# GpSimd's order in the attention written out, table scatters one to a round, and the first expert's weights split by VectorE

## The chip, the core and the metric

The kernel runs on one core of a Trainium2 chip. The metric is the device time of the core in microseconds, start to end; the median of three runs counts. The engines are TensorE (PE, with its weight loads listed as PEld), VectorE (DVE), ScalarE (ACT), GpSimd (POOL) and SyncE (SP), which here issues DMAs.

## The reference

```python
def _attn_ref(q, k, v):                     # each [8, 8, 576, 64]
    scores = scale * np.matmul(q, k.transpose(0, 1, 3, 2))
    mask = (pos // 64)[:, None] >= (pos // 64)[None, :]
    scores = np.where(mask, scores, -1000000000.0)
    attn = softmax(scores)
    return np.matmul(attn, v)
...
def _moe_ref(x, w_gate, w_output_gate, w1, w2):   # x [4608, 512], 8 experts
    logits = x @ w_gate
    e_idx = np.argmax(logits, axis=1)
    gate_w = softmax(logits)[rows, e_idx]
    eom = 1.0 / (1.0 + np.exp(-(x @ w_output_gate)))
    for e in range(E):
        mask = e_idx == e
        h = np.maximum(x[mask] @ w1[e], 0.0)      # 512 -> 1024
        ye = h @ w2[e]                            # 1024 -> 512
        out[mask] = gate_w[mask, None] * eom[mask, e, None] * ye
```

The attention's output, with the heads of a token side by side, is x. Each token goes to one expert, the one with the largest logit.

## The kernel before

**Attention.** The 8 batches of 8 heads are 32 pairs of heads, four to a batch. A pair is worked through in a software pipeline of 138 rounds (`NG`), four rounds to a pair; `round_of(g)` emits what each round holds: maxima for pair g // 4, exponentials for the pair one back, values for the pair two back, and the norm and turn of the pair three back. Float32 products are made of 16-bit halves. So a probability tile (`pc`, and `pcr` for the odd 64 rows) has a low part (`lpc`, `lpcr`, L258, in `lows`), and V a high and a low part (`vh` by ScalarE, `vl` by GpSimd, L152). GpSimd makes the low parts, one `lpcr`, five blocks of `lpc` and one `vl` to a pair; TensorE's value matmuls (L267 to L269) read them.

**Routing.** When a batch's x is there, `finish_batches` is put on the list `later`. It is a generator with the logits (L532 to L541), the largest one and its one-hot `oh` (L550 to L560), the place in the expert's queue (a matmul, L577 to L588), the slot `sli` and the gate `idg` (L599). At the end stands one scatter per 128 tokens, `tab_d<-idg,sli`, an indirect DMA issued by GpSimd (L604), which writes token number and gate to the table in HBM. `pay_later` takes a generator one step on in a round whose letter it yielded; None means any. Batches 0 and 1, 2 and 3, 4 and 5 are routed as joint groups of ten 128-token tiles, 6 and 7 alone, with five each.

**First expert.** `load_first`, put on `later` in round 120, loads the first expert's w1 and w2 in chunks. It reads the ids of the first tokens from the table (`fetch_ids`, L783, behind all scatters of the batches 0 to 5), gathers their rows of x (`fetch_x`, L794, into `xg`), and splits the weights into halves (`split`, L822 by ScalarE for the high part, L824 for the low part). `split` cuts a low part into quarters unless VectorE makes it. In rounds of `FIRST`, and behind the attention, the generator `ahead` is taken a step on: staging of tokens (L893 to L895), and h steps, the matmuls by w1 (L946).

**What sets the order.** Within `tc.manual_schedule` TensorE, ScalarE and VectorE work in the order in which the code emits; GpSimd and the DMA queues are ordered by a scheduler, from what its operations depend on. Behind the attention the experts' loop runs for the rest of the time.

Of the kernel before, what the change touches and what calls it, by code (L numbers as in the profile page):

```python
# [26 lines left out]
def block_attention_top1_moe(  # L27
# [11 lines left out]
    nc = tc.nc  # L39
    B, H, S, D = q.shape  # L40
# [459 lines left out]
    def pay_later(kind=None):  # L500
        for g in list(later):
            if kind is None or want.get(g) in (None, kind):
                want[g] = next(g, later)
                if want[g] is later:
                    later.remove(g)

    scatters, tab_reads = [], []
    GROUPS, Ls = ((0, 1), (2, 3), (4, 5), (6,), (7,)), {}
    ROUNDS = "ywab"

    def finish(b, xT):
        group = next(x for x in GROUPS if b in x)
        if b == group[0]:
            L = small.tile([P, len(group), NT, 16], F32, name="L", padded_shape=[P, 2, NT, 16])
            Ls[group] = L
        later.append(finish_batches(b, group, Ls[group], xT))

    def finish_batches(b, group, L, xT):

        n, b0 = len(group), group[0]  # L520
        joint = n > 1
        M = n * NT

        def tile_(shape, dt, name):
# [78 lines left out]
        for t in range(M):  # L603
            sc = nc.gpsimd.indirect_dma_start(  # L604
                out=tab_d, out_offset=IOA(ap=sli[:, t:t + 1].bitcast(U32), axis=0),
                in_=idg[:, b0 + t // NT, t % NT, :], in_offset=None, bounds_check=TROWS - 1, oob_is_err=False,
            ).ins
            if scatters:
                tc.declare_no_dep(sc, group="scatters", reason="distinct slots")
            for ins in tab_init + tab_reads:  # L610
                tc.add_manual_dep(sc, ins.name, SYNC, reason="after earlier accesses of the table")
            tc.add_to_no_dep_group("scatters", sc)
            scatters.append(sc)
            if b < B - 4:
                yield ROUNDS[t % 4]
            elif t % 2:
                yield


    def counts(col, name):  # L620
# [13 lines left out]
    def route_first():  # L634


        cnt = counts(B - 2, "cnt0")
        mx = small.tile([P, 1], F32, name="f_mx")
        nc.vector.tensor_reduce(mx, cnt, AX.X, ALU.max)
        eq = small.tile([P, E], F32, name="f_eq")  # L640
        nc.vector.scalar_tensor_tensor(eq, cnt, mx, erev, ALU.is_equal, ALU.mult)
        er = small.tile([P, 1], F32, name="f_er")
        nc.vector.tensor_reduce(er, eq, AX.X, ALU.max)
        nc.vector.tensor_scalar(first, erev, er, None, ALU.is_equal)
        fe = small.tile([P, 1], F32, name="f_e")
        nc.vector.tensor_scalar(fe, er, -1.0, float(E), ALU.mult, ALU.add)
        nc.vector.tensor_copy(f_i, fe)
        nc.vector.tensor_scalar(fe, fe, float(NTOK), None, ALU.mult)
        nc.vector.tensor_scalar(row0, t64[:, 0:8:2], fe, None, ALU.add)
# [4 lines left out]
    def sequence(order, i0, used):  # L654
        seq = []
        for i, kind in enumerate(order):
            k = KINDS.index(kind)
            seq.append((BKIND[k] + used[k], KTILES[k], i0 + i))
            width[i0 + i] = KROWS[k] // KTILES[k]
            used[k] += 1  # L660
        return seq

    used = [0] * len(KINDS)
    steps = sequence(ORDER, 0, used)
# [100 lines left out]
    @contextmanager  # L765
    def chain():
        if chained[0] is None:
            yield
        else:
            with tc.issue_after(chained[0].ins):  # L770
                yield


    def fetch_ids(st, halves=None):

        c, n, i = st
        if i not in ids:
            ids[i] = fs.tile([P, 2, 2], I32, name="ids", bufs=8)
        lo, hi = halves or (0, n)
        row = row0[0:1, 2 * c + lo:2 * c + lo + 1] if i < 2 else rti[0:1, c:c + 1]  # L780
        with tc.issue_after(read[0].ins) if read[0] else nullcontext():
            rv = nc.gpsimd.value_load(row, min_val=0, max_val=E * NTOK)
            read[0] = nc.gpsimd.dma_start(  # L783
                ids[i][:, lo:hi], tab_d[bass.ds(rv, P * (hi - lo)), :].rearrange("(h p) c -> p h c", p=P)
            )
        for sc in scatters:
            tc.add_manual_dep(read[0].ins, sc.name, SYNC, reason="after the scatters")
        tab_reads.append(read[0].ins)

    def fetch_x(st, halves=None):  # L790
        c, n, i = st
        for h in range(*(halves or (0, n))):
            nx = NTOK - 2 * S if 2 * i + h < 3 else NTOK
            nc.gpsimd.indirect_dma_start(  # L794
                out=xg[i % NXG][0:width[i], h], out_offset=None, in_=x_d[0:nx, :],
                in_offset=IOA(ap=ids[i][0:width[i], h, 0:1].bitcast(U32), axis=0), bounds_check=nx - 1, oob_is_err=False,
            )

    def rows_of(w, ev, j):

        n = 1024 // w.shape[2]
        rows = w.rearrange("e (g p) n -> e p g n", p=P)[bass.ds(ev, 1), :, n * j:n * (j + 1)]
        return rows.rearrange("e p g n -> (e p) g n")

    def quarter(w, t):
        return t.rearrange("p (g n) -> p g n", n=w.shape[2])
# [40 lines left out]
    def load_first():  # L847

        route_first()
        with chain():  # L850
            ev = nc.sync.value_load(f_i[0:1, 0:1], min_val=0, max_val=E - 1)

        wc = {}

        def load(w, c):
            dt, nm = ((F16, "hh"), (BF16, "hl"))[c % 2]
            wc[c] = fs.tile([P, KF, 2, P], dt, name=nm).rearrange("p f h n -> p (f h n)").bitcast(F32)
            nc.sync.dma_start(quarter(w, wc[c]), rows_of(w, ev, c))

        for c in range(4):  # L860
            load(w1, c)
        for r in "bwyab":
            yield r
        assert len(scatters) == (B - 2) * NT
        fetch_ids(steps[0])
        fetch_ids(steps[1], (0, 1))
        fetch_x(steps[0])
        fetch_x(steps[1], (0, 1))
        yield "w"
        for w, fn in ((w1, split_w1), (w2, split_w2)):  # L870
            for c in range(4):
                with tc.issue_after(last_exp[0].ins):
                    fn(nc.gpsimd, 0, wc[c], c)
                if w is w1:
                    load(w2, c)
                yield "yabw"[c]

    def buf(i):
        return 0 if i < 2 else (i - 1) % 2
# [179 lines left out]
    def round_of(g):  # L1059

        r = g % 4

        def do(back, name, *args):
            p, rr = divmod(g - back, 4)
            if 0 <= p < NPR:
                getattr(pairs[p], name)(*args)

        if r == 0:
            if g < 4 * NPR:
                max_odd(g // 4)  # L1070
            do(0, "max_tile", 0)
            do(4, "prob_tile", 3)
            do(12, "norm")
            do(4, "lows", 3)
        elif r == 1:
            do(5, "prob_tile", 0)
            do(5, "prob_tile", 1)
            do(1, "max_tile", 1)
            do(5, "lows", 0)
            do(5, "lows", 1)  # L1080
            if g == 4 * NPR + 9:
                turn_rest(NPR - 1, NPR)
        elif r == 2:
            do(6, "prob_tile", 2)
            do(10, "values_odd")
            do(2, "max_tile", 2)
            do(2, "max_rest")
            pay_later("m")
            pay_later("n")
            do(10, "values", 0)  # L1090
            pay_later("v")
            do(6, "lows", 2)
        else:
            do(-5, "turn")
            if g < 4 * NPR:
                turn_max(g // 4)
            if g < 4 * NPR + 8:
                turn_rest(g // 4 - 3, g // 4 + 2)
            pay_later("x")
            do(11, "values", 1)  # L1100
        for fn in events.get(g, ()):
            fn()
        pay_later("abwy"[r])

    NG = 4 * NPR + 10
    FIRST = range(NG - 6, NG)
    AT = mybir.EngineType
    with tc.manual_schedule(engines={AT.PE, AT.Activation, AT.DVE}):
        for g in range(NG):
            round_of(g)  # L1110
            if g in FIRST:
                next(ahead)
        while later:
            next(ahead, None)
            pay_later()
# [112 lines left out]
```

## Time and profile before

| what | value |
|---|---|
| runs | 821.64, 818.17, 815.3 us; median 818.17 us |
| profiled execution | 816.6 us, span 815.0 us |
| TensorE | 725.2 us busy, 89% of the span, mean granted clock 0.948 |
| VectorE, ScalarE, GpSimd | 533.8, 445.3, 415.5 us busy |

The attention takes about the first 400 us of the span. Busy shares are means over stages; the rows below are taken by stage. In a timeline's row stand the start, the duration, the engine, the line, the operation and its operands, the number of like instructions that the row joins, and in brackets the idle time ahead of it, with what ended it ("issue": nothing that the profile shows).

### The profile page before, as it was taken

The page shows a single profiled execution, that of the slowest core. Times are in us where ns is not written, and L with a number is a line of the kernel's source. Part 1 is how long each engine was busy: PE and PEld are TensorE (multiplying, and loading weights), DVE is VectorE, ACT ScalarE, POOL GpSimd, SP SyncE. Part 2 cuts the span into 40 slices and gives each one's busy share as a digit, 9 for nine tenths or more (in the row PEclk, how much of TensorE's full clock was granted, in tenths as well). Part 3 has the DMA queues.
Part 4 walks back from the last instruction along what each step waited for, and adds up shares of the span by engine and source line. Part 5 has one row for each costly group of instructions (what it writes and reads, how often), then busy time and mean ns, then how long its engine had stood idle before and what let it go on. Part 6 is the DMA issues. An engine that isn't in the chain of part 4 may idle for free. (4 is left out here: it accounts for less than half of the span.)

```text
span 815.0 us, 24272 instructions
## 1 busy us (share of the span) xinstructions
PE 725.2 (89%) x9879; PEld 536.3 (66%) x9879; DVE 533.8 (65%) x889; ACT 445.3 (55%) x630; POOL 415.5 (51%) x411
## 2 busy tenths in 40 slices
PE   5899998679985998976997799999999999999994
PEld 4687877458762777745874576956668566686651
DVE  7677778637784577727353796967678666796530
ACT  2676665346661665515220776855577655885530
POOL 3788787768867786459424644222333332220011
PEclk9999999979997899968798999999999999999998
DMA  6555655424544254325107799789999969941601
GB/s 155 130 132 139 143 135 123 105 53 116 144 102 90 62 131 101 103 64 157 31 1 250 179 264 305 240 254 308 322 303 353 314 167 297 229 112 43 230 27 43
DMA packets 207850, 131.61 MB, mean 161 GB/s; under 512 B 161552, under 2 KB 180016, under 8 KB 207728
## 3 DMA queue, kind: packets, MB, share of 16 engines
q1 hardware_dynamic: 199680, 110.66, 49.7%
q0 software_dynamic: 8048, 19.29, 7.6%
q8 instruction: 80, 1.31, 0.7%
q14 instruction: 42, 0.34, 0.2%
HBM read 127.08 MB, written 19.34 MB: 180 GB/s over the span
## 5 line engine op out<-in xcount | busy, mean ns | idle before, releaser
L946 PEld LDWEIGHTS <-w1b 128*128 128x128 f16 (+1 forms) x2208 | 177.1, 98 | 22.6 <-DVE w1b L824 1.1
L946 PE MATMUL ps_s<-xt,w1b 128*128 128x256 f16 (+5 forms) x1920 | 175.4, 253 | 0.8 <-issue 0.4
L975 PE MATMUL ps_o<-w2b,hh 128*128 128x512 f16 (+1 forms) x560 | 169.4, 384 | 4.4 <-ACT hh L954 4.4
L824 DVE TENSOR_TENSOR w2b<-w2f,w2b 128x1024 bf16<-128x1024 f32 x80 | 92.9, 1221 | 90.1 <-ACT w2b L822 75.9
L258 POOL TENSOR_TENSOR lpc<-pc 128x512 f16<-128x512 f32 x143 | 144.1, 1041 | 3.9 <-ACT pc L249 2.7
L984 POOL DMA_INDIRECT out_dram<-ys,ids x38 | 51.8, 1362 | 153.2 <-ACT ys L983 82.5
L178 DVE TENSOR_REDUCE nmz<-ps_s 128x2 bf16<-128x896 f32 (+3 forms) x128 | 82.6, 692 | 48.7 <-PE ps_s L194 47.2
L975 PE MATMUL ps_o<-w2b,hl 128*128 128x512 f16 x280 | 107.6, 384 | 0.2 <-DVE hl L955 0.2
L975 PEld LDWEIGHTS <-hh 128*128 128x128 f16 x560 | 55.2, 99 | 68.0 <-ACT hh L954 4.5
L824 DVE TENSOR_TENSOR w1b<-w1f,w1b 128x1024 bf16<-128x1024 f32 x80 | 92.8, 1219 | 1.5 <-ACT w1b L822 0.8
L983 ACT ACTIVATE ys<-ps_o,ids 128x512 f32<-128x512 f32 (+1 forms) x38 | 26.1, 686 | 111.8 <-PE ps_o L975 91.5
L249 ACT ACTIVATE pc<-ps_s 128x1024 f32<-128x1024 f32 (+1 forms) x96 | 78.4, 882 | 12.5 <-PE ps_s L213 12.4
L822 ACT CAST w1b<-w1f 128x1024 f16<-128x1024 f32 x80 | 78.4, 1045 | 4.4 <-DMA w1f<-in_moe_w_dram 4.3
L258 POOL TENSOR_TENSOR lpcr<-pcr 128x640 f16<-128x640 f32 x32 | 40.1, 1253 | 78.1 <-ACT pcr L249 78.1
L129 DVE TENSOR_TENSOR tr<-ps_s,tr 128x1024 f16<-128x1024 f32 (+1 forms) x62 | 47.1, 769 | 49.1 <-ACT tr L128 46.0
L822 ACT CAST w2b<-w2f 128x1024 f16<-128x1024 f32 x80 | 77.8, 1043 | 1.6 <-DMA w2f<-in_moe_w_dram 1.6
L794 POOL DMA_INDIRECT xg<-x_d,ids x38 | 54.3, 1429 | 36.6 <-DVE xr L908 12.7
L213 PE MATMUL ps_s<-tr,tr 64*128 64x512 f16 (+3 forms) x512 | 63.5, 314 | 9.6 <-issue 9.3
L249 ACT ACTIVATE pcr<-ps_s 128x640 f32<-128x640 f32 x32 | 22.5, 705 | 87.4 <-PE ps_s L241 42.4
L128 ACT CAST tr<-ps_s 128x1024 f16<-128x1024 f32 (+1 forms) x62 | 41.5, 670 | 41.9 <-PE ps_s L124 41.9
L187 PE MATMUL ps_s<-tr 64*128 64x384 f16 (+3 forms) x256 | 38.0, 314 | 26.7 <-DVE tr L129 22.2
L213 PEld LDWEIGHTS <-tr 64*128 64x128 f16 x768 | 35.4, 98 | 38.8 <-issue 28.0
(215 smaller groups left out, 1582.2 us busy)
## 6 DMA issues: line engine op xcount, KB each, us to landing
w1f<-in_moe_w_dram SPq DMA_DIRECT2D x80, 512.0 KB
w2f<-in_moe_w_dram SPq DMA_DIRECT2D x80, 512.0 KB
nat<-in_k_dram SPq DMA_DIRECT2D x64, 128.0 KB
nat<-in_q_dram SPq DMA_DIRECT2D x64, 128.0 KB
vn<-in_v_dram SPq DMA_DIRECT2D x64, 128.0 KB
x_d<-xn SPq DMA_DIRECT2D x32, 256.0 KB
vn<-in_v_dram SPq DMA_DIRECT2D x64, 32.0 KB
hh<-in_moe_w_dram SPq DMA_DIRECT2D x4, 512.0 KB
```

Of the source, the lines that this page charges most:

```text
L128: (hi or nc.scalar.copy)(th, ps)
L129: nc.vector.tensor_tensor(tl, ps, th, ALU.subtract)
L178: last_max[0] = nc.vector.tensor_reduce(o, ps[:, :, c0:c1], AX.X, ALU.max, negate=True)
L213: nc.tensor.matmul(os[ab], ks(kc, ab), qs(qc, ab), start=j == 0, stop=j == 3)
L249: last_exp[0] = nc.scalar.activation(self.pt[i], ap, AF.Exp, scale=SCALE)
L258: eng.tensor_tensor(self.pl[i][:, sl], self.pt[i][:, sl], self.high(i)[:, sl], ALU.subtract)
L794: nc.gpsimd.indirect_dma_start(out=xg[i % NXG][0:width[i], h], out_offset=None, in_=x_d[0:nx, :], in_offset=IOA(ap=ids[i][0:width[i], h, 0 ...
L822: nc.scalar.copy(hi, src)
L824: eng.tensor_tensor(lo[at], src[at], hi[at], ALU.subtract)
L946: nc.tensor.matmul(ph[:, f4].rearrange("p (h n) -> p h n", n=w), wv[:, cc, f, :], xv[:, cc], start=(k == 0), stop=(k == 3 * KD - 1))
L975: nc.tensor.matmul(py, hv[:, f, h], wv[:, f, :], start=(k == 0), stop=(k == 3 * KF - 1))
L984: nc.gpsimd.indirect_dma_start(out=out, out_offset=IOA(ap=ids[i][0:w, h, 0:1].bitcast(U32), axis=0), in_=ys[0:w], in_offset=None, bounds_c ...
```

## The change

- GpSimd is put under `tc.manual_schedule`, so its work in the attention stands in the order of the code.
- A scatter's generator yields a letter after every scatter: "abw" in turn, so one scatter in three of the four rounds of a pair (batch 5: "yabw", one in every round).
- Batches 4 and 5 are no longer one group; they are routed apart, with the letters of a joint group.
- `load_first` waits one round longer and fetches the ids; the low parts of the first expert's weights are made by VectorE, two to a round-letter's step, in whole chunks; the gathers `fetch_x` come after the first two chunks of w1.
- `FIRST` has four rounds instead of six: 132, 133, 136 and 137.

```diff
-    GROUPS, Ls = ((0, 1), (2, 3), (4, 5), (6,), (7,)), {}
-    ROUNDS = "ywab"
+    GROUPS, Ls = ((0, 1), (2, 3), (4,), (5,), (6,), (7,)), {}
...
-        joint = n > 1
+        joint = b < B - 2
...
-            if b < B - 4:
-                yield ROUNDS[t % 4]
-            elif t % 2:
-                yield
+            yield ("yabw"[t % 4] if b == B - 3 else "abw"[t % 3]) if joint else None
...
-        for r in "bwyab":
+        for r in "bwyabw":
             yield r
         assert len(scatters) == (B - 2) * NT
         fetch_ids(steps[0])
         fetch_ids(steps[1], (0, 1))
-        fetch_x(steps[0])
-        fetch_x(steps[1], (0, 1))
-        yield "w"
         for w, fn in ((w1, split_w1), (w2, split_w2)):
             for c in range(4):
                 with tc.issue_after(last_exp[0].ins):
-                    fn(nc.gpsimd, 0, wc[c], c)
+                    fn(nc.vector, 0, wc[c], c)
                 if w is w1:
                     load(w2, c)
                 yield "yabw"[c]
+                if w is w1 and c == 1:
+                    fetch_x(steps[0])
+                    fetch_x(steps[1], (0, 1))
...
-    FIRST = range(NG - 6, NG)
+    FIRST = (NG - 6, NG - 5, NG - 2, NG - 1)
-    with tc.manual_schedule(engines={AT.PE, AT.Activation, AT.DVE}):
+    with tc.manual_schedule(engines={AT.PE, AT.Activation, AT.DVE, AT.Pool}):
```

Line numbers behind L508 are smaller by one to four in the changed kernel: the scatter is L603, the ids read L779, the gather L790, the split L820.

GpSimd in the pairs 13 and 14, where batches 0 and 1 are scattered (`lpc` and `lpcr` are low parts, `vl` the low V, L604 the scatters), before:

```order
L258 TENSOR_TENSOR lpcr<-pcr 128x640
L258 TENSOR_TENSOR lpc_3770<-pc_3766 128x512 x2
L258 TENSOR_TENSOR lpc_3771<-pc_3767 128x512 x2
L258 TENSOR_TENSOR lpc_3772<-pc_3768 128x512
L152 TENSOR_TENSOR vl_104<-vn_99,vh_102 128x640
L604 DMA tab_d<-idg,sli 37120x2 x10
L258 TENSOR_TENSOR lpcr<-pcr 128x640
```

and now:

```order
L258 TENSOR_TENSOR lpcr<-pcr 128x640
L258 TENSOR_TENSOR lpc_3770<-pc_3766 128x512 x2
L258 TENSOR_TENSOR lpc_3771<-pc_3767 128x512 x2
L603 DMA tab_d<-idg,sli 37120x2
L258 TENSOR_TENSOR lpc_3772<-pc_3768 128x512
L152 TENSOR_TENSOR vl_104<-vn_99,vh_102 128x640
L258 TENSOR_TENSOR lpcr<-pcr 128x640
L603 DMA tab_d<-idg,sli 37120x2
L258 TENSOR_TENSOR lpc_4051<-pc_4047 128x512 x2
L258 TENSOR_TENSOR lpc_4052<-pc_4048 128x512 x2
L603 DMA tab_d<-idg,sli 37120x2
L258 TENSOR_TENSOR lpc_4053<-pc_4049 128x512
```

The ten scatters in a row have become single ones between low parts; the first has moved ahead of the pair's last low part and low V.

GpSimd at the attention's end, from the gathers (L794, now L790) on, before:

```order
L794 DMA xg_8327<-x_d,ids 128x512 x2
L794 DMA xg_8329<-x_d,ids 128x512
L152 TENSOR_TENSOR vl_103<-vn_98,vh_101 128x128
L824 TENSOR_TENSOR w1b_8325<-hh,w1b_8325 128x256 x4
L824 TENSOR_TENSOR w1b_8325<-hl,w1b_8325 128x256 x4
L258 TENSOR_TENSOR lpcr<-pcr 128x640
L824 TENSOR_TENSOR w1b_8325<-hh,w1b_8325 128x256 x4
L824 TENSOR_TENSOR w1b_8325<-hl,w1b_8325 128x256 x4
L152 TENSOR_TENSOR vl_104<-vn_99,vh_102 128x128
L824 TENSOR_TENSOR w2b_8326<-hh,w2b_8326 128x256 x4
```

and now, from the second ids read (L779) on:

```order
L779 DMA ids<-tab_d 128x2
L258 TENSOR_TENSOR lpcr<-pcr 128x640
L790 DMA xg_8379<-x_d,ids 128x512 x2
L790 DMA xg_8381<-x_d,ids 128x512
L778 TENSOR_LOAD row_199
L778 ISA x2
L152 TENSOR_TENSOR vl_104<-vn_99,vh_102 128x128
L603 DMA tab_d<-idg,sli 37120x2 x10
```

The weight quarters are gone from GpSimd, and the gathers have moved behind the last `lpcr`.

VectorE at the routing of one of the last batches, before:

```order
L541 TENSOR_REDUCE L<-ps_s 128x80
L301 TENSOR_SCALAR sm<-ps_v 128x10
L302 RECIPROCAL sm<-sm 128x10
L305 TENSOR_TENSOR xn<-ps_v,sm 128x2x2x64 x2
L305 TENSOR_TENSOR xn<-ps_v,sm 128x128
L550 TENSOR_REDUCE mx<-L 128x5
L553 TENSOR_TENSOR eq<-L,mx 128x40
```

and now:

```order
L820 TENSOR_TENSOR w1b_8377<-hh,w1b_8377 128x1024
L820 TENSOR_TENSOR w1b_8377<-hl,w1b_8377 128x1024
L540 TENSOR_REDUCE L<-ps_s 128x80
L301 TENSOR_SCALAR sm<-ps_v 128x10
L302 RECIPROCAL sm<-sm 128x10
L305 TENSOR_TENSOR xn<-ps_v,sm 128x2x2x64 x2
L305 TENSOR_TENSOR xn<-ps_v,sm 128x128
L820 TENSOR_TENSOR w1b_8377<-hh,w1b_8377 128x1024
L820 TENSOR_TENSOR w1b_8377<-hl,w1b_8377 128x1024
L549 TENSOR_REDUCE mx<-L 128x5
L552 TENSOR_TENSOR eq<-L,mx 128x40
```

Two low parts of whole chunks now stand ahead of the logits' sum (L540), and two ahead of the largest logit (L549).

## Rows read from the trace of the kernel before

**Rows 1.** The page's slices of 20.4 us: TensorE's busy tenths, granted clock.

```profile
PE   5899998679985998976997799999999999999994
...
PEclk9999999979997899968798999999999999999998
```

**Rows 2.** Windows: length, busy time (instructions) of PE, PEld, DVE, ACT, POOL, clock.

```profile
66.91:95.98 29.07, 27.58 (x624) 22.62 (x620) 20.91 (x44) 18.94 (x31) 22.97 (x21) 1.00 0.58 139
124.32:135.49 11.17, 9.13 (x210) 7.67 (x206) 10.36 (x23) 6.13 (x10) 7.66 (x8) 1.00 0.47 112
145.42:190.69 45.27, 32.31 (x624) 24.36 (x620) 24.52 (x50) 18.94 (x31) 32.80 (x31) 0.85 0.36 81
169.44:180.98 11.54, 10.87 (x209) 8.76 (x210) 5.87 (x11) 6.59 (x11) 7.65 (x7) 0.81 0.15 34
241.50:286.40 44.90, 33.20 (x624) 24.51 (x620) 24.53 (x50) 18.94 (x31) 32.71 (x31) 0.85 0.39 82
337.18:356.34 19.16, 13.36 (x208) 8.52 (x206) 8.66 (x31) 4.70 (x9) 9.50 (x10) 0.87 0.54 156
356.34:372.00 15.66, 15.46 (x165) 12.70 (x164) 3.67 (x8) 6.55 (x11) 10.21 (x13) 0.61 0.20 52
388.00:400.00 12.00, 11.55 (x84) 10.33 (x83) 5.19 (x18) 3.72 (x7) 9.45 (x13) 0.53 0.11 27
404.43:407.21 2.78, 2.78 (x30) 2.31 (x31) 0.08 (x1) 1.72 (x3) 0.00 (x0) 1.00 0.08 17
```

**Rows 3.** Timeline of GpSimd in a quiet pair, and the next pair's start.

```profile
66.91 1.25 POOL L258 TENSOR_TENSOR lpcr<-pcr 128x640 f16<-128x640 f32 x1 [1.28 <-ACT pcr L249]
68.22 5.04 POOL L258 TENSOR_TENSOR lpc<-pc 128x512 f16<-128x512 f32 x5
73.22 1.40 POOL L152 TENSOR_TENSOR vl<-vn,vh 128x640 f16<-128x640 f32 x1
75.89 1.25 POOL L258 TENSOR_TENSOR lpcr<-pcr 128x640 f16<-128x640 f32 x1 [1.28 <-ACT pcr L249]
```

**Rows 4.** Timeline of GpSimd: the first two and the last of ten scatters.

```profile
153.69 1.05 POOL L604 DMA_INDIRECT tab_d<-idg,sli  x1 [0.56 <-DVE idg L599]
155.05 1.01 POOL L604 DMA_INDIRECT tab_d<-idg,sli  x1 [0.30 <-issue]
...
165.30 0.97 POOL L604 DMA_INDIRECT tab_d<-idg,sli  x1 [0.30 <-issue]
```

**Rows 5.** Timeline of TensorE and ScalarE during these scatters.

```profile
163.59 0.62 PE L213 MATMUL ps_s<-tr,tr 64*128 64x512 f16 x2 [1.50 <-issue]
...
168.65 0.70 ACT L249 ACTIVATE pcr<-ps_s 128x640 f32<-128x640 f32 x1 [16.27 <-remote]
```

**Rows 6.** Timeline: a scatter after the third burst, value matmuls beside it and later.

```profile
357.75 1.00 POOL L604 DMA_INDIRECT tab_d<-idg,sli  x1 [0.16 <-DMA tab_d<-idg,sli]
...
359.49 4.53 PE L291 MATMUL ps_v<-vn,pc 128*128 128x65 f32 x20
...
391.04 4.53 PE L291 MATMUL ps_v<-vn,pc 128*128 128x65 f32 x20
```

**Rows 7.** Timeline of VectorE, GpSimd and TensorE from 372 us on.

```profile
372.89 13.75 DVE L553 TENSOR_TENSOR eq<-L,mx 128x40 f32<-128x40 f32 x1
377.10 2.34 PE L291 MATMUL ps_v<-vn,pc 128*128 128x65 f32 x20
384.05 2.54 POOL L824 TENSOR_TENSOR w2b<-hl,w2b 128x256 bf16<-128x256 f32 x4
...
387.52 0.21 PE L577 MATMUL ps_s<-oh,below 128*128 128x40 f16 x1 [8.08 <-DVE oh L560]
...
411.07 0.20 DVE L553 TENSOR_TENSOR eq<-L,mx 128x40 f32<-128x40 f32 x1
...
435.09 1.08 PE L893 MATMUL ps_o<-ident,xg 128*128 128x128 f32 x4 [5.62 <-DMA xg<-x_d,ids]
```

**Rows 8.** Timeline of TensorE: the first matmul of a pair that reads a low V.

```profile
77.64 0.21 PE L268 MATMUL ps_v<-vl,pcr 64*128 64x64 f16 x2
```

**Rows 9.** Groups by line: VectorE's low parts of expert weights, busy and mean ns.

```profile
L824 DVE TENSOR_TENSOR w1b<-w1f,w1b 128x1024 bf16<-128x1024 f32 x80 | 92.8, 1219 | 1.5 <-ACT w1b L822 0.8 <-issue 0.6
```

## The prediction

> **What bounds the kernel now.** I read the slices first. TensorE (PE) is the busy engine nearly everywhere, and there are dips: slices 7 and 8 (143 to 183 us), 12 and 13, 17 and 18, and 21 and 22 [rows 1]. The first three fall in the attention, and the granted clock of TensorE falls beside them. The windows put sizes to them. Three quiet pairs take 29.07 us, with TensorE busy for 27.58 of them; the same number of matmuls takes 45.27 and 44.90 us where the routing of batches 0 and 1, and of 2 and 3, ends; 19.16 us go by in what is one pair at batches 4 and 5 [rows 2]. Then I read GpSimd. In a quiet pair it computes the low parts for 7.7 us (1.25 + 5.04 + 1.40) of a cadence of 8.98 us and waits 1.28 us for ScalarE [rows 3]: it is close behind, and not the bound. In the long pairs it issues table scatters back to back, 0.97 to 1.05 us each, 0.30 us apart [rows 4].
>
> While they run, TensorE all but stops. Its gaps are marked "issue", no wait that the trace shows, and are up to 1.50 us; when it goes on, ScalarE's exponentials, 16.27 us late, hold it up once more [rows 5]. What stops it I can't read. It isn't scatters as such: with two more scatters after the third burst the same 20 value matmuls took 4.53 us, as they did 30 us later with no scatter, both at the low clock [rows 6]. So the burst, beside a dense stream of small matmuls, is what the stall goes with.
>
> The fourth dip in the attention is another thing. GpSimd subtracts weight quarters back to back to 386.6 us, and one 128x40 subtraction on VectorE, 0.20 us elsewhere, takes 13.75 us; it ends when GpSimd pauses. TensorE, done at 379.4 us, waits 8.08 us for the one-hot behind it [rows 7]. After both kinds of stall the clock is low: 0.61 of full speed over 356 to 372 us and 0.53 over 388 to 400 us [rows 2].
>
> The Trainium skill, "SBUF — State Buffer", "Who interferes with whom", says that a VectorE instruction with two SBUF inputs and a GpSimd instruction that reads SBUF lock each other out for one whole instruction. By that the wait would be at most one quarter, 0.64 us (2.54 for four); the row says 13.75 us, some 20 quarters, so the measurement decides here.
>
> **The change, part by part.** The sum is made against the profiled execution, 816.6 us (span 815.0, 1.6 around it), which lies 0.2% under the median, 818.17.
>
> *Scatters of batches 0 to 3.* They stand one to a round, three to a pair, between low parts. The three pairs from 145.42 us take 45.27 us. Without a stall I put them at 29.07 us plus what routing adds to a pair, 11.17 less 8.98, so 2.2: together 31.2 us [rows 2, 3]. 14.1 us are lost there, and 44.90 less 31.2, 13.7 us, at the second burst.
>
> What takes the stall's place is GpSimd's lag. Its work in these pairs is 22.97 us [rows 2] plus 10 scatters at 1.15 us (one with a gap of 0.15, half of the 0.30), 11.5 us. The first scatter now also stands before the last low part of pair 13 and waits there for the gates: GpSimd gets to it at about 150.7 us (145.42 + 1.25 + four parts of 1.01), the scatter started at 153.69 [rows 4], so 2.9 us, and queued behind it are the last low part, the low V and the next pair's. Sum: 37.4 us of GpSimd against 31.2 us. Of the 6.2 us, the low parts' slack takes 3.0: the low V is done at 74.62 us, and the first matmul that reads one comes at 77.64 [rows 3, 8]. 3.1 to 3.2 us become waits of TensorE. **Gain: 14.1 + 13.7 - 2 x 3.15 = 21.5 us.** (From 29.07 as the unhindered time it would be 25.7, and 19 if the routing costs twice as much.)
>
> *Batches 4 and 5*, now routed apart. The pair with the third burst takes 19.16 us against 9.7, the mean of the three quiet ones: 9.5 lost. The low clock after it has TensorE busy in 15.46 of 15.66 us at 0.61: 0.39 x 15.66 / 0.5 is 12.2 us at half speed, of which half, 6.1, would be saved; I take 5.5, for some of it is not matmul rate. Against that stand batch 4's own routing, 2.2 us at the price above, and a lag of 5 scatters to a batch, about 1. **Gain: 15.0 - 3.2 = 11.8 us.**
>
> *The first expert's low parts* go to VectorE: 16 quarters each of w1 and w2 leave GpSimd (32 x 0.64 = 20 us) and 8 operations of 1.22 us, 9.8 us, come to VectorE [rows 7, 9], two to a place. VectorE is busy for 3.67 of the 15.66 us from 356 us on [rows 2], so it has room. The wait of 8.08 us goes; late next is a routing step behind two splits, 2.4 us at most once, of which I take 1. The low clock over 388 to 400 us goes with the wait: 0.47 x 12 / 0.5 = 11.3 us at half speed, 5.6 saved. **Gain: 8.1 - 1 + 5.6 = 12.7 us;** from 3 (the splits hold the same chain for 2.4 us each, and the clock falls nonetheless) to 14.
>
> That same page of the Trainium skill speaks against this edit: two-input splits on VectorE are to lock GpSimd's low parts out. By that, GpSimd would lose 9.8 us at most; with 20 us of work taken off it there, the sum would stay.
>
> *Two h steps later.* A step is 24 matmuls, 2.78 us [rows 2]. Two of them leave the stretch ahead of the last routing, where TensorE is full, and go to where it waits for the gather, 5.62 us [rows 7]. Nothing gained if the chain of VectorE operations is late anyway, 5.6 if not: I take 2.
>
> *Without a price:* the ids reads and the gathers move by two or three rounds, behind the last scatters of batch 5 and ahead of or behind low part 31. The table's initial DMA moves behind pair 0's low V, where nothing reads it for 100 us, and the two cleared gather buffers go to round 120, about 2 us beside GpSimd's idle time. Their cover is GpSimd's slack; without it they cost up to 2 us.
>
> *What single scatters cost TensorE.* No row shows one among dense small matmuls. From below it is 0, the equal 4.53 us [rows 6]; a gain has no mechanism, as a scatter does no work for TensorE. From above it is 1.28 us, the pitch in the burst [rows 4], if TensorE stands as long as each lasts. I take 0.2, nearer to the rows where TensorE isn't slowed, for 30 scatters: **6 us.**
>
> Sum: 21.5 + 11.8 + 12.7 + 2 - 6 = 42. **816.6 - 42 = 774.6 us.**
>
> **Rivals.** *The stall follows each scatter, not the burst.* For it: the loss, 14 us, is 1.4 for each of 10 scatters, near the pitch. Against it: [rows 6]. Then 30 scatters cost 1.2 instead of 0.2, 30 us more; since TensorE is then the slower, GpSimd's lag (6.3) is hidden: 774.6 + 30 - 6.3 = **798 us.**
>
> The page named above has a rule that the time could go by as well: TensorE has ports of its own and waits on no engine, so a burst on GpSimd could not stop it. If something else in these pairs does, such as the loads under way, the 21.5 and 9.5 us stay lost while the lag is hidden; from the rows that is 774.6 + 31 - 6 (no price of single scatters) = **799.6 us**, a result like the one above.
>
> *VectorE holds the chain.* The four pairs of splits meet the routing and the norms of pairs 29 to 31, TensorE waits for the one-hot as before, and the clock falls: the 12.7 us aren't gained, **787 us**. For it: the order puts the splits directly ahead of these steps. Against it: VectorE's idle time.
>
> *Slower: the clock.* Each scattered gap keeps TensorE at 1.2 GHz through whole pairs instead of a short stretch after a burst. The nearest row is 169.44 to 180.98 us: at a mean of 0.81, 4.4 us at half speed, a pair took 11.54 us, and TensorE was busy for 10.87 of it [rows 2], against 8.98 for a quiet one. With 8.6 us of matmuls a pair, at half speed throughout it would take up to 17, so 3 to 8 us a pair, say 5. Over 9 to 10 pairs with scatters that is 45, on top of the first rival less the low clock that was saved, 798 + 45 - 11 = **832 us**. It decides once more than half of these pairs run at the low clock.
>
> *The change doesn't do what it says:* no, its order shows the scatters between the low parts and the splits on VectorE.
>
> **How the numbers follow.** Forecast, 774 us: 0.58, within 757 to 788 (unhindered pairs at 29.07: -4; single scatters free: -6; h steps: -4; GpSimd's lag hidden: -3; upwards routing, VectorE and single scatters at 0.4). A stall at each scatter, 798: 0.14. A stall that something else makes, 800: 0.08. VectorE: 0.10. Slower by the clock: 0.05. Something unnamed: 0.05. The range, 757 to 803, holds all but the slow case and the edges. A measurement of this kernel tells about 1% from no change, so faster is under 810 us: 0.87; within 1%: 0.07, the stall kept and something lost beside it; slower: 0.06.
>
> **What would show it.** In the profile after: the pairs with scatters at 10 to 11.5 us and no "issue" gaps of over 0.5 us on TensorE (right) or one such gap after each scatter (first rival); ScalarE's longest wait for scores under 4 us; the 128x40 subtraction back at 0.2 us; no stretch at 1.2 GHz between 140 and 400 us; GpSimd's low parts late by up to 3 us at the end of each batch pair's scatters. The prediction is wrong if TensorE waits for low parts in every pair, or if the tail from the last scatter to the first gather gets longer by more than the h steps give.

## The result, and the profile after

The changed kernel takes 790.14 us (median of 4 runs, 787.34 to 793.87) against 816.73 us before: a ratio of 0.9669, 95% interval 0.9607 to 0.9731, so 27 us are gained where 42 were forecast. The time lies within the range of 757 to 803 us, and 2 us above the 757 to 788 us to which the prediction gave a chance of 0.58. The profiled execution is 790.95 us, its span 789.1 us.

The slices of the changed kernel (19.7 us each) against [rows 1]:

```profile
PE   5899998989889687887985999999999999999994
...
PEclk9899999999999898995997999999999999999998
```

The dips of slices 7, 8 and 12 are gone; those at 13, 15, 18 and 21 are new or still there. The windows cut both runs at the starts of the same pairs on GpSimd, its `lpcr` (13, 19; 21, 27, 31; the end). Columns as in [rows 2]. Before:

```profile
145.42:219.04 73.62, 59.26 (x1237) 46.40 (x1233) 45.05 (x92) 37.88 (x62) 55.77 (x53) 0.91 0.44 103
241.50:314.74 73.24, 60.15 (x1237) 46.54 (x1233) 45.05 (x92) 37.88 (x62) 55.68 (x52) 0.91 0.46 101
314.74:374.91 60.17, 50.98 (x834) 39.11 (x828) 33.75 (x85) 26.68 (x44) 35.73 (x40) 0.83 0.32 89
374.91:815.00 440.09, 409.10 (x3520) 286.66 (x3518) 282.61 (x343) 244.22 (x304) 145.84 (x132) 0.96 0.67 203
```

After, with two stretches of the end:

```profile
147.21:208.32 61.11, 55.59 (x1237) 45.05 (x1233) 43.13 (x92) 37.87 (x62) 55.81 (x52) 1.00 0.49 107
229.41:298.35 68.94, 58.72 (x1255) 46.42 (x1251) 53.60 (x114) 38.98 (x65) 59.74 (x56) 0.95 0.49 109
298.35:349.32 50.97, 43.57 (x820) 34.73 (x815) 36.13 (x83) 26.82 (x45) 25.51 (x26) 0.93 0.39 92
349.32:789.10 439.78, 409.50 (x3497) 288.16 (x3517) 275.03 (x349) 243.02 (x303) 122.64 (x110) 0.96 0.67 204
360.00:380.00 20.00, 19.83 (x138) 17.10 (x139) 4.72 (x14) 2.99 (x7) 4.97 (x5) 0.58 0.10 30
390.00:400.00 10.00, 7.35 (x103) 6.22 (x103) 2.78 (x11) 1.19 (x2) 4.89 (x5) 1.00 0.02 3
```

The first burst's pairs give 12.5 us, the second's only 4.3, the pairs of batches 4 and 5 give 9.2, and from the last pair on the gain is 0.3 us, where 12.7 and 2 were forecast. Pair 13 starts 1.8 us later than before, a loss that had no term; pairs 19 to 21 give 1.4.

GpSimd where the first group is scattered (timeline of the changed kernel):

```profile
153.67 1.07 POOL L603 DMA_INDIRECT tab_d<-idg,sli  x1 [1.12 <-DMA vn<-in_v_dram]
...
157.12 1.25 POOL L258 TENSOR_TENSOR lpcr<-pcr 128x640 f16<-128x640 f32 x1
158.56 1.03 POOL L603 DMA_INDIRECT tab_d<-idg,sli  x1 [0.18 <-issue]
...
168.40 1.25 POOL L258 TENSOR_TENSOR lpcr<-pcr 128x640 f16<-128x640 f32 x1
```

A pair now takes 11.28 us on GpSimd, with no pause ahead of `lpcr` (1.28 us in [rows 3]). In the second group's pairs and behind them VectorE and TensorE show what that does:

```profile
254.64 2.32 DVE L552 TENSOR_TENSOR eq<-L,mx 128x40 f32<-128x40 f32 x1
257.58 2.97 DVE L559 TENSOR_TENSOR oh<-er,erev 128x40 f16<-128x40 f32 x1
261.85 0.51 PE L187 MATMUL ps_s<-tr 64*128 64x384 f16 x2 [4.93 <-DVE tr L129]
303.38 3.84 DVE L552 TENSOR_TENSOR eq<-L,mx 128x40 f32<-128x40 f32 x1
309.34 0.50 PE L187 MATMUL ps_s<-tr 64*128 64x384 f16 x2 [4.25 <-DVE tr L129]
```

The compare that took 13.75 us in [rows 7] is short at its old place, but its sisters for batches 4 and 5, routed apart now, fall where GpSimd scatters the group ahead of them. And at the end:

```profile
342.63 0.98 POOL L603 DMA_INDIRECT tab_d<-idg,sli  x1 [0.30 <-issue]
347.50 0.75 POOL L779 DMA_DIRECT2D ids<-tab_d  x1 [3.89 <-DMA tab_d<-idg,sli]
354.32 1.38 POOL L790 DMA_INDIRECT xg<-x_d,ids  x1 [3.73 <-issue]
358.35 1.09 PE L889 MATMUL ps_s<-ident,xg 128*128 128x128 f32 x4 [4.53 <-DMA xg<-x_d,ids]
...
397.39 0.22 PE L942 MATMUL ps_s<-xl,w1b 128*128 128x128 bf16 x1 [1.07 <-issue]
```

TensorE waits for gathered rows in place of the one-hot, and the low clock (0.58 over 360 to 380 us) is there again, 20 us long. From the end of the last scatter ahead of the ids to the first gather it takes 10.7 us (343.61 to 354.32). Before, it took 5.7 us:

```profile
359.05 0.99 POOL L604 DMA_INDIRECT tab_d<-idg,sli  x1 [0.30 <-issue]
...
365.73 1.06 POOL L794 DMA_INDIRECT xg<-x_d,ids  x1 [0.90 <-DMA ids<-tab_d]
```

### The profile page after: what moved, and what is told of

Same layout as the page of the kernel before. It is cut to its first block, busy times and chain, and to the rows that moved or that the text cites. A ratio compares the mean times of both kernels' runs of the same rounds, so it can differ in the third digit from the quotient of the medians.

```text
span 789.1 us, 24243 instructions
## 1 busy us (share of the span) xinstructions
PE 713.5 (90%) x9859; PEld 532.0 (67%) x9880; DVE 534.2 (68%) x916; ACT 445.2 (56%) x632; POOL 384.1 (49%) x379
## 5 line engine op out<-in xcount | busy, mean ns | idle before, releaser
L971 PE MATMUL ps_o<-w2b,hh 128*128 128x512 f16 (+1 forms) x539 | 163.4, 382 | 8.9 <-ACT hh L950 8.7
L820 DVE TENSOR_TENSOR w2b<-w2f,w2b 128x1024 bf16<-128x1024 f32 x80 | 92.7, 1221 | 90.8 <-ACT w2b L818 87.0
L980 POOL DMA_INDIRECT out_dram<-ys,ids x38 | 46.5, 1223 | 160.5 <-ACT ys L979 83.3
L820 DVE TENSOR_TENSOR w1b<-w1f,w1b 128x1024 bf16<-128x1024 f32 x80 | 92.8, 1218 | 2.9 <-ACT w1b L818 2.8
L790 POOL DMA_INDIRECT xg<-x_d,ids x38 | 48.8, 1284 | 40.1 <-issue 13.8
L187 PE MATMUL ps_s<-tr 64*128 64x384 f16 (+3 forms) x256 | 37.4, 310 | 27.0 <-DVE tr L129 25.1
L213 PE MATMUL ps_s<-tr,tr 64*128 64x512 f16 (+3 forms) x512 | 60.1, 313 | 0.0
L603 POOL DMA_INDIRECT tab_d<-idg,sli x40 | 39.6, 989 | 41.4 <-DVE idg L598 32.2
L267 PE MATMUL ps_v<-vh,pc 128*128 128x65 f16 x572 | 59.1, 195 | 0.5 <-issue 0.5
```

The costliest lines, as they stand in the source:

```text
L213: nc.tensor.matmul(os[ab], ks(kc, ab), qs(qc, ab), start=j == 0, stop=j == 3)
L267: nc.tensor.matmul(o, hi, self.vh[rows, j], start=first, stop=False)
L790: nc.gpsimd.indirect_dma_start(out=xg[i % NXG][0:width[i], h], out_offset=None, in_=x_d[0:nx, :], in_offset=IOA(ap=ids[i][0:width[i], h, 0 ...
L820: eng.tensor_tensor(lo[at], src[at], hi[at], ALU.subtract)
L971: nc.tensor.matmul(py, hv[:, f, h], wv[:, f, :], start=(k == 0), stop=(k == 3 * KF - 1))
L980: nc.gpsimd.indirect_dma_start(out=out, out_offset=IOA(ap=ids[i][0:w, h, 0:1].bitcast(U32), axis=0), in_=ys[0:w], in_offset=None, bounds_c ...
```

## The experiments

The runs were made in four groups, each on one chip and with the kernel before beside it. That took 805.7, 818.8, 806.6 and 806.0 us (medians), the changed kernel 790.14 with the prediction's result and 788.91 in the second group. Variants of the changed kernel are therefore compared with it by time, and under 2 us is taken as nothing. The changed kernel itself was not run in the other three groups, so that its time is the same there is not shown; four variants on two of these chips, at 788.93 to 790.87 us, fit that. Beside a kernel before of 806 us the change would then gain 16 us and not 27. What makes the kernel before 12 us faster in those groups no run shows.

**The changed kernel again.** 

> The changed kernel once more, on the chip of the three runs beside it. Its GpSimd keeps a cadence of 11.2 us a pair while it scatters, VectorE's first compare of batch 4 and of batch 5 is held for over 2 us, and TensorE waits over 4 us for the gathered rows: 787 to 794 us. If the cause of these waits were chance, they would not be there again.

788.91 us (ratio 0.9631, 0.9569 to 0.9693). The waits are there again: 4.95 and 4.58 us behind held compares, 4.14 us for gathered rows. The variants are read against both.

**The burst put back where it was.**

```diff
-        yield
+        yield "w" if b < B - 3 else None
         for t in range(M):
...
-            yield ("yabw"[t % 4] if b == B - 3 else "abw"[t % 3]) if joint else None
+            if b >= B - 3:
+                yield "yabw"[t % 4] if joint else None
```

> The changed kernel with the scatters of batches 0 to 4 back to back, 10, 10 and 5, behind the pair's low V, where they stood in the kernel before. Theory A (a burst stops TensorE): gaps marked issue, 0.7 to 1.5 us each, at the bursts, and some 13 us between the pair starts more than in a quiet pair: 798 to 808 us. Theory B (a burst only holds up the low parts behind it, and the stall of the kernel before came from its loads): no such gaps, TensorE waits for a low part of 5 to 8 us at each burst at most, 785 to 796 us.

817.18 us, 28 us slower than the changed kernel beside it. Window of the pair with ten scatters, and one of TensorE's gaps at the second burst:

```profile
148.12:171.89 23.77, 12.56 (x213) 7.70 (x209) 11.43 (x24) 6.22 (x11) 17.61 (x17) 0.80 0.41 89
```

```profile
259.86 0.26 PE L213 MATMUL ps_s<-qe,kext 64*128 64x128 bf16 x1 [1.21 <-issue]
```

The pair takes 23.77 us again (24.02 before, from 145.42 to 169.44 us) and the gaps are back, with GpSimd in written order and all loads of the changed kernel: theory A, though the time lies 9 us above its range. The burst is the cause; on this chip its order alone is worth 28 us.

The run shows one thing more. Batch 4 is routed apart here as well, beside low parts that follow each other without a gap, but no scatters stand between them:

```profile
282.35 3.04 POOL L258 TENSOR_TENSOR lpc<-pc 128x512 f16<-128x512 f32 x3
283.77 0.67 DVE L552 TENSOR_TENSOR eq<-L,mx 128x40 f32<-128x40 f32 x1
284.48 0.96 DVE L553 TENSOR_TENSOR eq<-eq,erev 128x40 f32<-128x40 f32 x1
```

The same compare takes 0.67 us instead of 2.32: it ends with the second of the three low parts, and the next operation with the third. So neither the low parts as such nor the separate routing hold VectorE for long; the long holds come with the scatters between the low parts, with which GpSimd runs behind.

**The burst ahead of the low parts.** As above, but without the "w", so the scatters stand ahead of the pair's last low part.

> The changed kernel with the scatters of batches 0 to 4 issued back to back again, 10, 10 and 5, all else as changed. Theory A (a burst stops TensorE, single scatters don't): gaps marked issue on TensorE come back at each burst, the pairs with the two bursts of ten take 12 to 14 us longer than unhindered ones, while GpSimd's lag and VectorE's long waits behind it go: 795 to 808 us. Theory B (something else in these pairs of the kernel before stopped TensorE, the loads under way or the order of GpSimd): no gaps, and without the lag 778 to 786 us.

804.92 us. No gap of over 0.6 us marked issue, but a wait of TensorE at each burst of ten:

```profile
167.28 0.21 PE L268 MATMUL ps_v<-vl,pcr 64*128 64x64 f16 x1 [10.40 <-POOL vl L152]
```

Neither theory: TensorE has nothing to do while the scatters run, so it can't be seen to stall. This run told nothing of the stall; the scatters delay the low V, and TensorE waits for that.

**Two scatters to a pair.** `"abw"[t % 3]` becomes `"aw"[t % 2]`.

> The changed kernel with two scatters to a pair instead of three for batches 0 to 4. Theory A (three scatters keep GpSimd busy without a pause, 11.2 us a pair, and VectorE's small subtractions and compares with two inputs wait for its next pause: 2.32, 2.97 and 3.84 us instead of 0.20, so TensorE waits 4.93 and 4.25 us and its clock falls behind them): 10.0 us of GpSimd's work a pair, pauses in most pairs, each of these operations under 1.5 us, the two waits of TensorE under 2 us together, 780 to 785 us. Theory B (each scatter costs TensorE time by itself, wherever it stands): as many scatters, no gain, 788 to 793 us.

788.93 us, no gain. GpSimd's starts of two pairs, and the compare of batch 5:

```profile
168.19 1.25 POOL L258 TENSOR_TENSOR lpcr<-pcr 128x640 f16<-128x640 f32 x1
...
178.18 1.26 POOL L258 TENSOR_TENSOR lpcr<-pcr 128x640 f16<-128x640 f32 x1
```

```profile
306.42 5.20 DVE L552 TENSOR_TENSOR eq<-L,mx 128x40 f32<-128x40 f32 x1
```

The work is 10.0 us a pair as expected, but still over the quiet cadence of 8.98, so there is no pause either, and the compare is held for 5.20 us. That fits theory A's mechanism and refutes its number; theory B gave the same time. This run doesn't part them; the next does.

**Batches 4 and 5 as one group.**

```diff
-    GROUPS, Ls = ((0, 1), (2, 3), (4,), (5,), (6,), (7,)), {}
+    GROUPS, Ls = ((0, 1), (2, 3), (4, 5), (6,), (7,)), {}
...
-            yield ("yabw"[t % 4] if b == B - 3 else "abw"[t % 3]) if joint else None
+            if b != B - 3:
+                yield "abw"[t % 3] if joint else None
+            elif t % 2:
+                yield "yabw"[t // 2 % 4]
```

> The changed kernel with batches 4 and 5 routed as one group again, two scatters to a round at its end. Theory A (the compares of batch 4 and of batch 5 fall where GpSimd scatters the group ahead of them and never pauses): no routing stands in those pairs any more; the two waits of TensorE of 4 to 5 us and the low clock behind them go, 8 to 14 us, against which up to 6 us of later ids stand: 4 to 10 us faster than the changed kernel beside it. Theory B (the separate routing is worth it, as the prediction had it, since ten scatters at the end cost more): 3 us slower or more.

791.09 us. Windows of pairs 21 to 27 and 27 to 31, first of the changed kernel's second run, then of this one:

```profile
231.97:300.90 68.93, 57.71 (x1257) 46.10 (x1253) 54.96 (x114) 39.05 (x65) 59.76 (x57) 0.98 0.49 104
300.90:350.67 49.77, 42.02 (x817) 33.95 (x812) 37.38 (x83) 26.32 (x45) 25.46 (x27) 0.97 0.40 94
```

```profile
232.95:293.14 60.19, 55.54 (x1237) 44.71 (x1233) 43.13 (x92) 38.10 (x62) 55.76 (x52) 1.00 0.53 113
293.14:350.33 57.19, 48.11 (x879) 39.22 (x873) 40.22 (x99) 29.99 (x50) 29.52 (x31) 1.00 0.46 114
```

The six pairs take 60.19 us, as those of the first group do in the changed kernel (61.11): with no routing beside the scatters no compare is held over 1 us, and the pairs take 8.7 us less. All of it is given back at the end (the second window ends where GpSimd, after the wait shown next, comes to low part 31):

```profile
348.50 0.76 POOL L782 DMA_DIRECT2D ids<-tab_d  x1 [8.59 <-DMA tab_d<-idg,sli]
```

```profile
358.19 1.09 PE L892 MATMUL ps_s<-ident,xg 128*128 128x128 f32 x4 [9.37 <-DMA xg<-x_d,ids]
```

The last scatter is issued at 338.92 us, and GpSimd waits 8.59 us for it to land. So theory A holds for the pairs. In total neither theory does, with 2.2 us more than the changed kernel beside it: the end is bound by something else.

**Gathers early.** `fetch_x` stands right behind `fetch_ids` again.

> The changed kernel, with the three gathers put back right behind the ids reads, ahead of the last odd low part. Theory A (the ids land late because the loads of w2 fill the DMA queues from 346 to 354 us, so the gathers could not start before 353.6 us wherever they stand): no gain; the last odd low part queues behind them and starts some 5 us later, 0 to 5 us slower than the changed kernel (790 to 795 us). Theory B (the gathers are late because they stand behind the low part and two splits): TensorE's wait of 4.53 us for gathered rows goes and the low clock behind it with it, 8 to 10 us faster (780 to 782 us).

789.65 us, no change. GpSimd's first gather and TensorE's wait:

```profile
354.34 1.88 POOL L790 DMA_INDIRECT xg<-x_d,ids  x1 [5.32 <-DMA ids<-tab_d]
...
358.83 1.09 PE L888 MATMUL ps_s<-ident,xg 128*128 128x128 f32 x4 [5.42 <-DMA xg<-x_d,ids]
```

The gather starts at the same time as in the changed kernel: the ids were not there before. Theory A; the place of the gathers is not the reason. The last odd low part starts at 358.99 us instead of 349.32, and the time is no longer for it.

**The loads of w2 held.**

```diff
-            nc.sync.dma_start(quarter(w, wc[c]), rows_of(w, ev, c))
+            ld_ = nc.sync.dma_start(quarter(w, wc[c]), rows_of(w, ev, c))
+            if w is w2:
+                tc.add_manual_dep(ld_.ins, gathered[-1].name, SYNC, reason="after the gathers")
...
+            for r in "ya" if w is w2 else "":
+                yield r
...
-                if w is w1:
+                if w is w1 and c > 1:
                     load(w2, c)
...
+                    load(w2, 0)
+                    load(w2, 1)
```

> The changed kernel with the four loads of the first expert's w2 held until the third gather has landed, and its splits two steps later. Theory A (these loads delay the ids and the gathered rows): the ids land within 3 us of the read, TensorE's wait of 4.53 us for gathered rows falls to 0 to 1 us, the clock doesn't fall behind it; 6 to 10 us faster than the changed kernel (780 to 784 us), unless VectorE then waits for w2. Theory B (the gathers are late by their place behind the low part and the splits): the wait stays at 4 us or more, 788 to 794 us.

784.69 us, 4 to 5 us faster. Windows of 345 to 355 us, the changed kernel's and this one's (last columns: DMA share, GB/s), and this one's gather and wait:

```profile
345.00:355.00 10.00, 8.51 (x137) 7.43 (x125) 8.85 (x22) 8.02 (x13) 3.28 (x4) 1.00 0.99 238
```

```profile
345.00:355.00 10.00, 9.67 (x150) 8.53 (x149) 7.14 (x14) 8.46 (x14) 5.85 (x6) 1.00 0.13 32
```

```profile
353.45 1.86 POOL L790 DMA_INDIRECT xg<-x_d,ids  x1 [0.15 <-POOL lpcr L258]
...
357.85 0.63 PE L898 MATMUL ps_s<-ident,xg 128*128 128x128 f32 x4 [0.85 <-DMA xg<-x_d,ids]
```

With DMA at 0.13 instead of 0.99 the ids are there when GpSimd gets to the gather, and TensorE waits 0.85 and 0.89 us instead of 4.53. The profiled execution is the slowest of the four (788.39 us), and TensorE comes to that wait 3.2 us later than in the changed kernel (357.00 against 353.82 us), which makes it shorter too. The chain is shorter all the same: from the end of the last scatter to this matmul it takes 11.1 us instead of 14.7. Theory A. The clock still fell later (0.66 over 360 to 380 us), and the gain is less than the 6 to 10 us expected.

**The splits alone**, in the kernel before (`nc.gpsimd` becomes `nc.vector`, nothing else).

> The kernel before with only the first expert's low parts moved to VectorE, in whole chunks; scatters, groups and gathers as before. Theory A (the held compare of 13.75 us was GpSimd's subtractions back to back, and the gathers are early there): the compare takes 0.2 us, TensorE's wait of 8.08 us goes, and with it most of the low clock behind: 9 to 13 us faster than the kernel before. Theory B (something else is late at the same place): a new wait of 4 us or more takes its place, 0 to 5 us faster.

803.60 us against 818.83 (ratio 0.9803, 0.9739 to 0.9867): 15 us faster, 2 more than theory A's range. The compare, and the window that stands in [rows 2] with a clock of 0.53:

```profile
377.39 0.20 DVE L553 TENSOR_TENSOR eq<-L,mx 128x40 f32<-128x40 f32 x1
```

```profile
388.00:400.00 12.00, 12.00 (x113) 10.19 (x112) 2.56 (x6) 3.06 (x6) 4.83 (x5) 0.97 0.11 26
```

Theory A: the held compare was GpSimd's subtractions, and the gathers are early there.

**The splits back on GpSimd**, in the changed kernel.

> The changed kernel with the first expert's low parts back on GpSimd in quarters, in the written order: two chunks of w1 ahead of the last odd low part, all else as changed. Theory A (the splits' move is worth as much here as alone, 15 us, and only other things of the change ate it at the attention's end): the last odd low part, the gathers behind 10 us of quarters and VectorE's compare of batch 6 are late, TensorE waits 8 us or more there: 799 to 808 us. Theory B (with gathers and low clock as they are now, nothing hangs on the splits): 787 to 793 us.

790.17 us, as the changed kernel. VectorE and TensorE:

```profile
350.89 6.44 DVE L571 TENSOR_TENSOR run_cnt<-run_cnt,add 128x8 f16<-128x8 f16 x1
...
361.53 2.00 PE L889 MATMUL ps_s<-ident,xg 128*128 128x128 f32 x8 [5.59 <-ACT zs L574]
366.68 0.21 PE L268 MATMUL ps_v<-vl,pcr 64*128 64x64 f16 x1 [2.99 <-POOL vl L152]
```

Theory B by the time: inside this change the move of the splits is worth nothing. The rows show that this is a balance and not an absence: VectorE is held again, 6.44 us, but the loads of w2 come later (DMA share 0.14 over 345 to 355 us, 0.99 in the changed kernel). In this execution, the slowest of the four (794.72 us), TensorE waits 5.59 and 2.99 us, more than the 4.53 us in the changed kernel; where the median gets that back is not shown.

**Six rounds of early staging**, as before.

> The changed kernel with all six rounds of the end in the list of early token stagings and h steps, as before. Theory A (two h steps ahead of the last routing delay the last batch's chain, and TensorE has nothing to do while it waits for the last gather): 2 to 6 us slower, 791 to 796 us. Theory B (the chain is bound elsewhere): within 1.5 us of the changed kernel, 787 to 791 us.

790.87 us, 0.7 and 2.0 us over the two medians: too little to tell the theories apart. TensorE does wait there, at a place where the changed kernel has no wait:

```profile
411.21 1.09 PE L889 MATMUL ps_o<-ident,xg 128*128 128x128 f32 x4 [7.88 <-DMA xg<-x_d,ids]
```

**Joint routing and held loads together.**

> The changed kernel with batches 4 and 5 as one group, two scatters to a round, and with the loads of w2 held until the third gather has landed, their splits two steps later. Theory A (joint routing brings the last pairs 8 us forward, and what ate it was the last scatters' and the ids' landing behind the loads of w2, 8.6 us): the wait for the last scatter falls from 8.6 to some 3 us, TensorE's wait for gathered rows from 9.4 to under 4 us, 777 to 784 us. Theory B (the end of the scatters, ids and gathers is bound by their own chain, whatever the loads do): the wait stays over 7 us, 786 to 792 us.

780.85 us (771.59 to 782.96), the fastest; the two other variants in its group (the splits back, and the six rounds) took 790.17 and 790.87, 9 to 10 us more on the same chip. GpSimd's wait for the last scatter and TensorE's for gathered rows:

```profile
341.24 0.75 POOL L782 DMA_DIRECT2D ids<-tab_d  x1 [3.25 <-DMA tab_d<-idg,sli]
...
348.67 1.09 PE L901 MATMUL ps_s<-ident,xg 128*128 128x128 f32 x4 [3.89 <-DMA xg<-x_d,ids]
```

8.59 us have become 3.25, and 9.37 have become 3.89: theory A.

**The same, held for the ids alone** (the dependence is on the second ids read).

> The run with joint routing and held loads, but the loads of w2 wait only for the second ids read and not for the gathers. Theory A (what the loads delay are the last scatters and the ids; three gathers of 256 KB each get through beside them): VectorE gets w2 some 5 us earlier, batch 6's scatters move forward by 2 us or more, TensorE's wait for gathered rows stays under 5 us: 776 to 781 us. Theory B (gathers are delayed by the loads as much): TensorE's wait for gathered rows grows to 6 us or more, 782 to 787 us.

781.01 us (779.93 to 781.74; ratio 0.9679, 0.9649 to 0.9709), no difference. Batch 6's scatters start at 356.54 instead of 360.02 us, as theory A had it, but

```profile
349.34 1.09 PE L901 MATMUL ps_s<-ident,xg 128*128 128x128 f32 x4 [7.10 <-ACT w2b L824]
```

and 2.38 us more for the next gathered rows. The wait has the size that theory B gave, the time lies at the edge of theory A's. The row names ScalarE's high part of w2 as what ended the first wait, so whether that or the gathered rows held TensorE isn't shown. GpSimd's wait for the last scatter is 5.47 us here, with the loads of w2 still held (DMA share 0.24 over 335 to 340 us and 0.03 over 340 to 345): how long a scatter takes to land is not a matter of these loads alone.

## Why the prediction was right in sign and off by 16 us

*The stall goes with the burst, not with each scatter:* right, and shown by the burst put back, which costs 28 us on its chip. Single scatters leave no gap marked issue of over 0.8 us in the changed kernel's attention; in two variants one gap of 1.0 us stands beside a scatter (the loads held, at 302.61 us; the six rounds, at 301.61). The row from which the prediction took it couldn't show it: its 20 float32 matmuls start at 359.49 us, when one of the two scatters is over and the other half done [rows 6], and in the changed kernel even five scatters in a row leave such matmuls alone (364 to 370 us). The first group's six pairs take 61.11 us; unhindered I would put them at 31.2 plus the 28.35 us that pairs 16 to 19 took before (73.62 less 45.27 of [rows 2]), 59.6. So 1.5 us remain for ten scatters and GpSimd's lag together, where 2 + 3.15 were forecast. Both rivals on the stall, at 798 and 800 us, are out.

*GpSimd's lag:* its cadence, 11.28 us a pair, was right (34.5 us for three by the forecast's terms), and its price as a wait for low parts too high: none of over 0.7 us in the changed kernel, one or two of 1.2 to 2.1 us in the pairs with scatters of six variants. The bracket beside the term, 25.7 or 19 us from another unhindered time, doesn't follow: three pairs bound by GpSimd take 37.4 - 3.0 = 34.4 us whatever TensorE would need, so the gain stays at 21. What the step left out is what a GpSimd that is behind does to VectorE. The row that shows it was read, the compare of 13.75 us, but only as a matter of the weight quarters, and "late next" was looked for in that place alone. The low parts do the same where scatters put GpSimd behind; a scatter itself does not (under one, at 271.53 us of the changed kernel, a two-input operation takes 0.17 us). The Trainium skill, "SBUF — State Buffer", "Who interferes with whom", says that VectorE's two-input instructions and GpSimd's reading ones block each other fully, for the length of one instruction. The runs agree on the pair. On the length they agree where GpSimd is not behind, 0.67 and 0.96 us with the burst put back; where it is behind they don't: holds of 2.3 to 6.44 us, several GpSimd instructions of 1 us each or quarters of 0.64. Why the hold goes on there no run shows.

*Batches 4 and 5:* the step that failed most in the attention. Routing batch 4 by itself was priced at 2.2 us, the price in pairs where GpSimd pauses. It costs 8.7 us in the pairs 21 to 27 (68.93 against 60.19), through that batch's two held operations (2.32 and 2.97 us in the first profile, and TensorE's wait of 4.93 behind them) and the clock behind those. The gain forecast, 11.8, was 9.2 at pairs 27 to 31, less these 8.7. Joint routing was no better in sum because its ten scatters landed late. With the loads held in both it is worth 3.8 us (784.69 against 780.85, on two chips); where the rest of the 8.7 goes was not followed.

*The splits on VectorE:* the term, 12.7 us, was right as a term; alone it measured 15. In the sum it gave 0.3 together with the h steps, because the line "without a price: the ids reads and the gathers" was wrong. VectorE frees the chunk buffers earlier, so the 2 MB of w2 come at 345 to 355 us, beside the last scatters, the ids and the gathered rows (DMA share 0.99). The ids are late, TensorE waits 4.53 us, and the low clock that was to go, 5.6 us, is there at 360 to 380 us. I asked what the splits wait for and not what they trigger. That these loads are one cause is shown, that they are the whole of it is not: holding them back gave 4 to 5 us of the 12.7. Of the two ways in which the forecast could go on this term, the rival that the chain is held (787 us) came near in its time by luck; its mechanism, VectorE too busy, did not come true.

*The h steps:* 2 us forecast; between 0.7 and 2 measured, within what can't be told from nothing. A wait of 7.88 us for gathered rows is filled by them.

*What had no term:* pair 13 starts 1.8 us later than before. With GpSimd in written order that start varies from 145.08 (the loads held for the ids) to 148.29 us (the loads held); with the splits alone it is 145.33 us. What causes it was not tried.

*Its signs:* the first group's pairs at 9.9 to 11.3 us and the compare of 0.20 us at its old place (351.82 us) came as foretold, and gaps marked issue of over 0.5 us all but went (one of 0.77 us beside a scatter). Two came out against it. The clock falls to its low level once more before 400 us (0.58 over 360 to 380 us). And the tail from the last scatter to the first gather is 5.0 us longer, more than the 2 us of the h steps, which the prediction had named as a sign that it is wrong.

What stays open is why TensorE stops at a burst, and why VectorE is held for more than one instruction of a GpSimd that is behind.

## What to carry to other kernels

When a change lets an engine free buffers sooner, ask which loads that starts, and what small transfers (scatters, ids, gathered rows) then queue behind them; here holding 2 MB back a few microseconds and routing two batches jointly gave 8 to 9 us more. Spread work into an engine's idle time only as far as some idle time is left: an engine that no other waits for, but that runs behind without a pause, held the small operations of another one for up to 5 us, where it held them for under 1 us when it was not behind. A term measured alone and the same term inside a change can differ by all of it, so price each freed wait by what is late next.

## What the runs showed of the hardware

- A burst of indirect DMAs stopped TensorE where it works through many small matmuls. In the changed kernel five scatters at 391.65 to 397.8 us go with gaps of 1.07 and 1.04 us among 128x128 matmuls, with a DMA share of 0.02 over 390 to 400 us: loads under way are not needed. The second gap begins as the last scatter ends. The five at 364 to 370 us, beside some 5 float32 matmuls a microsecond at a clock of 0.50, go with none.
- GpSimd waited 8.59 us for its last table scatter to land beside the loads of w2, and 2.87 to 5.47 us in the runs where these came later.
- VectorE's two-input operations of 0.20 us, down to 128x8 elements, took up to 6.44 us beside low parts or quarters of a GpSimd that was behind (13.75 us before), and 0.67 to 0.98 us beside the same low parts where it was not.
- The kernel before took 805.7 to 818.8 us in the four groups of runs (medians), each on one chip. The changed one took 790.14 and 788.91 us, both times beside a kernel before of 817 to 819 us; beside one of 806 us it was not run.
